# A fused attention and gated-MLP kernel: the hand-written order of all five engines is laid out anew

## Chip, core and metric

One core of one Trainium2 chip. The metric is device time in microseconds (us); less is better. The kernel before has a median of 278.79 us over three runs (279.18, 276.15 and 278.79).

## What is computed

Eight batches, twelve heads, 448 positions, head dimension 64. Queries and keys are RMS-normalised, then softmax attention, then a gated MLP with a spatial mix:

```python
q_n, k_n = rmsnorm(q, g_q), rmsnorm(k, g_k)
attn = softmax(q_n @ k_n.T / 8)                 # per head, 448 x 448
x = (attn @ v) laid out as (batch, 448, 768)
h = relu(x @ w_in)                              # 768 -> 1024
u, v = h[..., :512], h[..., 512:]
v_n = (v - mean(v)) / sqrt(var(v) + 1e-6)
v_s = w_spatial @ v_n + b_spatial               # mixes positions
out = (u * v_s) @ w_out                         # 512 -> 768
```

## The kernel before

All data of a batch is cut into 3 groups of 4 heads, so there are 24 groups G (batch G // 3). Nothing is scheduled by a compiler. A string, `PLAN`, is a list of 1,658 words; the kernel goes through it once, and each word issues the instructions of one step. Every engine runs its own instructions strictly in the order in which their words stand, and so do the DMA queues of SP (most transfers) and of POOL (the `v` and weight loads). Waits between engines come from the data and the buffers. A word is `name.arguments/slots/engine`; the engine is `a` (ACT), `v` (DVE) or `g` (POOL), and slots are buffer numbers: PSUM banks 0 to 7, or buffers of a pool (10 `raw`, 3 `sqt`, 4 `nrm`, 2 `kr`, 22 `et`, and so on).

The steps of a group G, with i = 0 for queries and 1 for keys:

- `L.G.i` loads q or k (SP, 448 KB), `Q` squares it into `sqt` (ACT, DVE or POOL), `R` sums the squares (DVE), `I` and `J` make 1/rms by a logarithm and an exponential (ACT), `N` multiplies into `nrm` (POOL or DVE). Group 0 has the same steps in two halves, in small letters (`l q r i j n p k`).
- The transpose to head dimension by position is done for groups 0 to 3 on TensorE (`P`, or `p`) with a copy out of PSUM (`K`, `k`), and from group 4 on by a DMA transpose on SP (`T.G.i`); `Z.G` then scales the transposed keys (DVE or ACT).
- `S.G.u` computes the scores of a seventh of the keys for the group's four heads (8 matmuls of 64x32 tiles; group 0 is cut otherwise), `E.G.u` is its exponential (ACT, PSUM to `et`). `s`, `a` and `b` sum those over the keys: `s` with ones, `a` and `b` with the two halves of V. From group 4 on two groups share these passes (`s.8.1.1` is for groups 8 and 9).
- `D` and `d` make the reciprocal of the sum (ACT), `X.G.half` multiplies (DVE, PSUM to `xt`). `v.b.n` is a load of a part of V of batch b (POOL, 112 or 224 KB).

The steps of a batch b: `V` and `W` (tail rows) and `U` are matmuls with `w_in`; `c` and `u` the relu copies out of PSUM; `B` the mean and variance; `M`, `m`, `A` the normalisation; `H` the spatial mix; `G` the gating; `O` the matmul with `w_out`; `o` its copy out of PSUM; `t.b.m` the store on SP (two DMAs of 64 rows each). `Y` and `y` transpose `w_spatial` at the start.

`z.n/f` issues n dummy matmuls of 64 columns on TensorE; nothing reads them.

[...]

```python
    def port(eng, inst):
        other = on_port.get("g" if eng is dve else "v")
        if other is not None:
            sync_dep(inst, other)
        on_port["v" if eng is dve else "g"] = inst
```

Of the kernel before, what the change touches and what calls it, by code (L numbers as in the profile page):

```python
# [27 lines left out]
y.0//a K.1.1/1/v S.1.5/45 S.1.1/23 Q.2.0/0/a R.2.0//v v.1.3//g L.2.1/5 S.1.6/67 Q.2.1/2/a wi.1.1//g E.1.5/2/a  # L28
wi.0.1//g Y.1/0 p.1.1/5 E.1.6/3/a R.2.1//v S.1.3/67 s.1.6.0/4 y.1//v k.0.1//v I.2//a wi.0.3//g E.1.1/4/a J.2//a
L.4.1/6 k.1.1//v E.1.3/5/a S.1.2/01 E.1.2/6/a s.1.5.0 a.1.1.0/5 S.0.3/23 s.1.3.0 N.2.1/2/v E.0.3/7/a S.1.4/67  # L30
E.1.4/8/a L.3.0/7 a.1.6.0 L.3.1/8 s.1.1.0 S.1.0/01 a.1.5.0 P.2.1/3 N.2.0/3/v P.2.0/2 L.6.1/9 wi.1.3//g wi.1.2//g
E.1.0/9/a Q.3.0/1/v S.0.6/67 K.2.1/2/v wi.0.0//g Q.3.1/0/g R.3.0//v s.1.2.0 b.1.1.0/3 S.0.2/01 b.1.6.0 a.1.2.0 s.1.0.0
wb Q.4.1/2/g K.2.0/2/v b.1.4.0 E.0.6/a/a s.1.4.0 R.3.1//v wi.1.0//g S.2.2/67 E.0.2/b/a D.1/0/a L.4.0/0 a.1.0.0 a.1.4.0
s.0.0.0/2 Q.4.0/1/v E.2.2/c/a S.0.4/01 E.0.4/d/a a.1.3.0 wi.0.2//g s.0.6.0 I.3//a s.0.1.0 b.1.0.0 L.5.1/3 d.1//a
Q.6.1/0/v b.1.2.0 X.1.0//v S.0.5/67 J.3//a v.1.1//g S.2.1/01 s.0.3.0 N.3.0/0/g s.0.2.0 b.1.3.0 a.0.6.0/4 a.0.1.0
b.1.5.0 E.0.5/e/a v.1.2//g X.1.1//v E.2.1/f/a S.2.0/56 E.2.0/g/a a.0.4.0 s.0.5.0 b.0.3.0/7 L.6.0/2 s.0.4.0 R.4.0//v
S.2.4/01 b.0.0.0 b.0.2.0 a.0.3.0 E.2.4/h/a b.0.5.0 L.7.0/1 a.0.0.0 a.0.5.0 L.5.0/5 s.2.1.0/6 S.2.3/01 b.0.1.0
Q.5.1/1/a P.3.0/5 R.4.1//v R.6.1//v N.3.1/1/g P.3.1/3 a.0.2.0 E.2.3/i/a Q.5.0/2/g S.2.6/01 K.3.0/3/v b.0.6.0 I.4//a
s.2.4.0 K.3.1/3/v D.0/1/a J.4//a E.2.6/j/a N.4.0/2/g b.2.1.0/5 L.7.1/4 S.3.0/23 R.5.0//v b.2.0.0 s.2.2.0 E.3.0/k/a
S.2.5/01 E.2.5/l/a R.5.1//v wx//v s.2.0.0 d.0//a T.4.0/1 s.2.3.0 b.2.6.0 b.2.2.0 s.2.6.0 X.0.0//v b.0.4.0 S.3.1/23  # L40
E.3.1/4/a b.2.4.0 a.2.0.0/0 s.2.5.0 a.2.5.0 a.2.3.0 a.2.4.0 I.5//a a.2.1.0 N.4.1/3/g T.4.1/0 S.3.4/12 D.2/0/a J.5//a
b.2.5.0 a.2.2.0 X.0.1//v E.3.4/3/a b.2.3.0 N.5.1/0/v T.5.1/1 S.3.3/34 N.5.0/1/g a.2.6.0 S.3.2/67 U.0.2.0/2 V.0.1.1/1
d.2//a V.0.1.0 X.2.1//v V.0.2.1/5 X.2.0//v V.0.1.2 T.5.0/0 U.0.2.1 Q.6.0/0/a U.0.2.2 R.6.0//v Z.4/1/v V.0.2.0
E.3.2/8/a S.4.2/67 E.3.3/9/a L.9.0/7 c.0.1//v I.6//a J.6//a N.6.1/2/g S.4.0/34 B.0.1//v u.0.2//a Z.5/0/v E.4.2/6/a
S.4.1/01 W.0/2 E.4.0/5/a E.4.1/2/a S.4.5/67 c.0.3//v S.4.4/34 E.4.4/1/a Q.7.0/2/v L.8.0/8 E.4.5/7/a V.0.2.2 c.0.2//v
U.0.0.0/2 U.0.0.1 S.5.6/01 E.5.6/0/a S.5.1/34 L.10.0/0 E.5.1/d/a U.0.0.2 U.0.3.2/5 U.0.3.1 S.5.0/67 u.0.0//v S.5.5/01
S.3.5/34 V.0.0.2/2 Q.7.1/1/g E.5.0/a/a U.0.3.0 V.0.0.0 E.3.5/b/a V.0.0.1 S.5.4/67 S.3.6/34 E.5.5/e/a s.3.0.0/1
R.7.1//v R.7.0//v I.7//a s.3.5.0 Q.9.0/0/g a.3.0.0/0 s.3.1.0 N.6.0/3/g s.3.2.0 Q.8.0/1/g L.11.0/6 u.0.3//v E.5.4/g/a
a.3.3.0 J.7//a S.5.2/56 B.0.2//v b.3.2.0/7 T.6.1/0 E.3.6/h/a s.3.3.0 a.3.5.0 E.5.2/f/a S.4.6/34 a.3.4.0 L.8.1/3
b.3.5.0 B.0.3//v c.0.0//v B.0.0//v s.3.6.0 E.4.6/l/a a.3.6.0 s.3.4.0 D.3/1/a b.3.0.0 a.3.2.0 S.4.3/56 T.6.0/2 S.5.3/23  # L50
L.10.1/5 N.7.1/0/g T.7.1/1 a.3.1.0 M.0//a E.4.3/c/a s.4.6.1/41 R.8.0//v v.2.2//g L.14.0/9 E.5.3/i/a s.4.1.1 m.0//a
Z.6/2/v N.7.0/1/g s.4.2.1 s.4.5.1 b.3.1.0 S.6.1/56 E.6.1/j/a A.0.1//v s.4.4.1 b.3.6.0 A.0.0//v A.0.2//v s.4.0.1
A.0.3//v s.4.3.1 b.3.4.0 b.3.3.0 d.3//a X.3.1//v D.4/0/a S.6.4/23 Q.8.1/2/g X.3.0//v U.0.1.2/5 U.0.1.0 U.0.1.1 H.0.0/4
E.6.4/b/a R.9.0//v G.0.0//v wo//g H.0.3/0 v.2.0//g G.0.3//v u.0.1//a H.0.1/6 S.6.3/23 S.6.0/45 b.4.6.1/07 b.4.4.1
b.4.0.1 d.4//a Z.7/3/a G.0.1//v D.5/1/a b.4.5.1 b.4.2.1 R.8.1//v b.4.3.1 a.4.4.1/61 E.6.0/k/a S.6.2/45 E.6.3/8/a
Q.10.0/1/g a.4.5.1 a.4.0.1 a.4.6.1 T.7.0/3 E.6.2/4/a d.5//a L.9.1/2 b.4.1.1 a.4.2.1 I.8//a R.10.0//v a.4.1.1 a.4.3.1
v.2.1//g S.7.0/23 X.4.1//v Q.10.1/0/g S.7.3/45 V.1.2.0/0 E.7.0/h/a X.4.0//v J.8//a N.8.1/2/g T.8.1/0 H.0.2/6 V.1.1.0/3
X.5.1//v X.5.0//v E.7.3/3/a G.0.2//v S.7.5/12 S.7.2/45 Q.9.1/2/v R.9.1//v S.7.4/67 V.1.2.2 E.7.5/9/a N.8.0/3/g
E.7.2/1/a V.1.2.1 T.8.0/1 c.1.2//a V.1.0.1/1 E.7.4/g/a L.11.1/4 V.1.0.0 V.1.0.2 W.1/045 S.6.5/67 c.1.0//a R.10.1//v
I.10//a o.0.3.1/0/v S.6.6/12 o.0.3.0//a c.1.3//v V.1.1.2 S.7.1/45 I.9//a J.9//a N.9.1/0/g T.9.1/1 U.1.1.0/0 U.1.1.2  # L60
E.6.5/7/a J.10//a E.6.6/e/a V.1.1.1 N.9.0/1/v U.1.0.1/7 S.7.6/12 U.1.1.1 Z.8/1/v E.7.6/5/a c.1.1//v U.1.0.0 U.1.0.2
O.0.1.0/6 E.7.1/a/a u.1.0//v u.1.1//v B.1.3//v S.8.1/12 S.8.3/34 s.6.0.1/57 E.8.1/0/a s.6.1.1 s.6.2.1 N.10.1/2/g
N.10.0/3/g s.6.3.1 B.1.0//v s.6.4.1 E.8.3/l/a s.6.5.1 s.6.6.1 T.9.0/0 S.8.2/01 U.1.3.0/2 U.1.3.1 Q.11.0/1/a Q.11.1/2/g
T.10.1/0 L.14.1/1 B.1.2//v U.1.2.0/3 D.6/0/a R.11.0//v B.1.1//v U.1.3.2 E.8.2/6/a O.0.1.1/4 u.1.3//v T.10.0/2
o.0.1.0/1/a U.1.2.1 d.6//a O.0.0.0/5 M.1//a D.7/1/a U.1.2.2 L.12.0/3 o.0.0.0/2/v o.0.1.1//a S.8.0/01 L.13.1/8 m.1//a
b.6.0.1/26 Z.9/0/v b.6.1.1 E.8.0/f/a b.6.2.1 u.1.2//v b.6.3.1 S.8.5/45 A.1.0//v b.6.4.1 L.13.0/2 d.7//a b.6.5.1
A.1.2//v b.6.6.1 E.8.5/2/a S.9.1/01 A.1.1//v O.0.0.1/7 X.7.1//v E.9.1/d/a L.12.1/7 Q.14.0/0/g L.18.1/5 S.9.4/34
# [689 lines left out]
```

## Time and profile before

The profiled execution took 275.98 us, of which its span (first to last instruction) is 274.2 us.

| | busy us of the span | instructions |
|---|---|---|
| TensorE matmul (PE) | 257.9 | 4372 |
| ScalarE (ACT) | 217.8 | 357 |
| VectorE (DVE) | 203.8 | 355 |
| GpSimd (POOL) | 145.0 | 122 |
| DMA, all queues | 51.14 MB, 187 GB/s mean | |

Durations of one instruction, from the groups of the page, that are used below:

| step | engine and form | mean ns |
|---|---|---|
| `E` | ACT, 128x896 out of PSUM | 923 |
| `N`, `Q` | POOL, 128x896 | 1691, 1683 |
| `N`, `Q` | DVE, 128x896 | 1088, 1086 |
| `R` | DVE | 1076 |
| `c`, `u` | DVE | 683, 619 |
| `c`, `u` | ACT | 591, 548 |
| `o` | DVE, ACT | 555, 491 |
| `Z` | DVE, ACT | 471, 1071 |
| `n` | DVE, POOL | 616, 950 |

How to read it: the span is a sum of stages with different limits. In the first 45 us attention of batch 0 is made, and no MLP matmul can start. From then to about 223 us attention of later batches and the MLP of earlier ones are interleaved. After that only MLP steps are left, and after 268.9 us only copies and stores. The busy time of PE is not PE at its peak, since matmuls overlap one another.

### The profile page before, as it was taken

Reading aid. Unit: us, or ns where it says so; the run is one execution under the profiler, and the core shown is the slowest. Engines: PE = TensorE matmul, PEld = TensorE weight load, DVE = VectorE, ACT = ScalarE, POOL = GpSimd, SP = SyncE. Lnnn points to the kernel's source line nnn. Section 1 sums busy time; section 2 is a strip of 40 time slices with the busy share of each in tenths; the row PEclk is TensorE's granted clock in tenths of the full one; section 3 lists DMA queues with packets and bytes.
Section 4 is the critical chain, followed back from the end, with each engine's and each line's share of the span. In section 5 each row is a group of like instructions: output and inputs, shape, how many; then the busy total and the mean of one; then the engine's idle time right before and its main releaser. Section 6 shows DMA issues by size and latency. Waiting matters only on the chain.

```text
span 274.2 us, 10148 instructions
## 1 busy us (share of the span) xinstructions
PE 257.9 (94%) x4372; PEld 137.5 (50%) x4389; DVE 203.8 (74%) x355; ACT 217.8 (79%) x357; POOL 145.0 (53%) x122
## 2 busy tenths in 40 slices
...
GB/s 208 319 344 273 260 171 119 295 204 245 167 145 168 376 177 187 198 251 184 232 184 267 286 246 241 175 95 61 194 114 141 117 2 2 31 29 115 154 279 204
DMA packets 63072, 51.14 MB, mean 187 GB/s; under 512 B 39601, under 2 KB 58674, under 8 KB 63026
## 3 DMA queue, kind: packets, MB, share of 16 engines
...
q8 instruction: 34, 0.56, 0.8%
q14 instruction: 12, 0.10, 0.1%
...
## 4 chain that ended last, share of the span: by engine, by line
PE 42%; POOL 13%; DMA 12%; DVE 10%; ACT 10%; issue 10%; SPq 1%; ACTq 0%; POOLq 0%; DVEq 0%
PE ps L551 8%; PE ps L690 7%; POOL nrm L438 7%; PE ps L662 7%; DMA vt<-in_v_dram 6%; ACT et L526 6%; PE ps L676 6%; PE ps L596 5%; PE ps L518 5%; POOL sqt L394 5%; DMA raw<-in_q_dram 3%; DVE ss L405 3%; DMA kr<-nrm 3%; PE ps L625 3%; POOL vt L326 2%
## 5 line engine op out<-in xcount | busy, mean ns | idle before, releaser
L526 ACT ACTIVATE et<-ps 128x896 bf16<-128x896 f32 x168 | 146.1, 923 | 13.4 <-PE ps L518 11.4
L438 POOL TENSOR_TENSOR nrm<-raw,rs 128x896 bf16<-128x896 f32 x40 | 67.3, 1691 | 29.0 <-ACT rs L423 9.4
L518 PE MATMUL ps<-qT,kT 64*32 64x448 bf16 x1344 | 61.1, 357 | 3.2 <-DVE kT L476 1.1
L551 PE MATMUL ps<-et,vt 64*32 64x448 bf16 x1344 | 52.1, 350 | 2.5 <-DMA vt<-in_v_dram 1.0
L394 POOL TENSOR_TENSOR sqt<-raw 128x896 f32<-128x896 f32 x28 | 46.8, 1683 | 13.8 <-DVE vn L653 9.3
L405 DVE TENSOR_REDUCE ss<-sqt 128x14 f32<-128x896 f32 x46 | 48.5, 1076 | 2.9 <-ACT sqt L392 1.2
L662 PE MATMUL ps<-xt,w_in 128*128 128x448 bf16 x192 | 43.4, 353 | 0.2
L518 PEld LDWEIGHTS <-kT 64*32 64x32 bf16 x1344 | 22.2, 90 | 31.7 <-issue 22.5
L690 PE MATMUL ps<-w_out,gt 128*128 128x384 bf16 x192 | 36.5, 326 | 0.1
L580 DVE TENSOR_TENSOR xt<-ps,rc 128x448 bf16<-128x448 f32 x48 | 27.9, 618 | 11.5 <-ACT rc L574 6.9
L596 PE MATMUL ps<-w_in,xt 128*128 128x512 bf16 x127 | 33.9, 380 | 0.9 <-issue 0.3
L551 PEld LDWEIGHTS <-vt 64*32 64x32 bf16 x1344 | 24.9, 92 | 16.2 <-issue 4.2
L373 ACT ACTIVATE os<-ps 128x384 f32<-128x384 f32 (+1 forms) x34 | 16.3, 491 | 15.2 <-PE ps L690 14.6
L551 PE MATMUL ps<-et,ones 64*32 64x448 bf16 x672 | 27.8, 349 | 0.0
L676 PE MATMUL ps<-w_spT,vn 128*128 128x448 bf16 (+1 forms) x128 | 27.7, 353 | 0.2 <-DVE xt L580 0.2
L662 PEld LDWEIGHTS <-w_in 128*128 128x128 bf16 x192 | 17.2, 97 | 20.8 <-issue 7.4
L690 PEld LDWEIGHTS <-gt 128*128 128x128 bf16 x192 | 18.1, 98 | 15.6 <-issue 2.7
L681 DVE TENSOR_TENSOR gt<-ps,us 128x448 bf16<-128x448 f32 x32 | 19.2, 619 | 9.0 <-PE ps L676 5.9
L637 DVE BATCH_NORM_STATS2 s<-vs 128x6 f32<-128x512 bf16 (+1 forms) x32 | 21.9, 683 | 1.6 <-ACT vs L587 1.1
L375 DVE COPY os<-ps 128x384 f32<-128x384 f32 (+1 forms) x30 | 16.5, 555 | 8.9 <-PE ps L690 5.5
L326 POOL DMA_DIRECT2D vt<-in_v_dram x34 | 23.0, 681 | 0.0
L589 DVE TENSOR_SCALAR vs<-ps 128x512 bf16<-128x512 f32 (+1 forms) x24 | 16.3, 683 | 7.4 <-PE ps L596 3.5
...
## 6 DMA issues: line engine op xcount, KB each, us to landing
...
w_in<-in_moe_w_in_dram POOLq DMA_DIRECT2D x8, 192.0 KB, 12.8
...
```

Source lines behind the costliest of these rows:

```text
L326: pool.dma_start(out=vts[b % 2][64 * halves[0]:64 * halves[0] + 64 * len(halves), g].rearrange("p r c d -> p r (c d)"), in_=src)
L394: port(eng, eng.tensor_tensor(out=t, in0=x, in1=x, op=ALU.mult))
L405: dve.tensor_reduce(out=sss[G % 3][:, i].rearrange("p r c -> p (r c)"), in_=sqt[where.pop(("sq", G, i))].rearrange("p r (c d) -> p (r c) d ...
L438: port(eng, eng.tensor_tensor(out=nrm[sl[0]].rearrange("p c r d -> p r c d"), in0=raw[where["raw", G, i]].rearrange("p r (c d) -> p r c d" ...
L518: pe.matmul(out=ps[at:at + 32, sl[n], 0:S], lhsT=kT[64 * r:64 * r + 64, c, 64 * hh + 32 * x:64 * hh + 32 * x + 32], rhs=qT[64 * r:64 * r + ...
L526: act.activation(out=ets[sl[0]], in_=ps[:, a:b + 1:b - a, 0:S], func=AF.Exp, bias=0.0, scale=1.0)
L551: pe.matmul(out=ps[32 * l:32 * l + 32, where[kind, G][0], 0:S], lhsT=w, rhs=et_of(G, r, c)[at:at + 64], start=(n == 1), stop=(n == C), til ...
L580: dve.tensor_tensor(out=xts[b % 2][:, 2 * g + half, :], in0=ps[:, where.pop(("ab"[half], G))[0], 0:S], in1=rcs[where["rc", G]], op=ALU.mult)
L596: pe.matmul(out=ps[:, bank, :], lhsT=xts[b % 2][:, j, 128 * m:128 * m + 128], rhs=w_in[:, j % 2, j // 2, DH:], start=(n == 1 and j == 2 * ...
L662: pe.matmul(out=ps[:, bank, 0:S], lhsT=w_in[:, j % 2, j // 2, 128 * f:128 * f + 128], rhs=xts[b % 2][:, j, :], start=(n == 1 and j == 2 * ...
L676: pe.matmul(out=ps[:, sl[0], 0:S], lhsT=vns[b % SLOTS["vn"]][rows, m, 128 * f:128 * f + 128], rhs=w_spT[rows, m, :], start=(m == 0), stop= ...
L690: pe.matmul(out=ps[:, sl[0], 0:384], lhsT=gts[b % 2][:, f, 128 * m:128 * m + 128], rhs=w_out[:, f, 384 * h:384 * h + 384], start=(f == 0), ...
```

## The change

The whole string `PLAN` is replaced by another order with the same 1,658 words; only the order, the slots and some engine letters differ, and the numbers in the `z` words. No other line changes. Counted by engine letter:

| step | before | after |
|---|---|---|
| `N` | 40 POOL, 6 DVE | 34 POOL, 12 DVE |
| `Q` | 28 POOL, 13 ACT, 5 DVE | 30 POOL, 9 ACT, 7 DVE |
| `n` | 2 POOL, 2 DVE | 4 DVE |
| `q` | 4 ACT | 3 ACT, 1 DVE |
| `k` | 4 DVE | 3 DVE, 1 ACT |
| `y` | 2 ACT, 2 DVE | 4 DVE |
| `Z` | 17 DVE, 3 ACT | 16 DVE, 4 ACT |
| `c` | 24 DVE, 8 ACT | 19 DVE, 13 ACT |
| `u` | 22 DVE, 10 ACT | 23 DVE, 9 ACT |
| `o` | 30 DVE, 34 ACT | 27 DVE, 37 ACT |
| dummies in `z` | 140 | 111 |

The diff, cut to the start, to some lines around batch 3's V loads, and to the end. Since every line of the string differs, words have to be looked for, not lines:

```diff
-setup//v l.1.0/0 gl.0//g z.1/f q.1.0/0/a l.0.0/1 z.5/f q.0.0/1/a z.11/f l.0.1 q.0.1//a z.1/f z.3/f z.11/f gl.1//g
-l.1.1 z.5/f z.1/f L.1.1/2 r.1.0//v r.0.0//v i.0//a L.1.0/3 j.0//a q.1.1//a gA//v z.1/f z.35/f r.0.1//v n.0.0//v
-Q.1.1/2/a z.34/f n.1.0//v z.9/f Q.1.0/1/a z.23/f r.1.1//v gB/2 gC//v i.1//a p.0.0/4 k.0.0/0/v p.1.0/0 k.1.0/0/v
-S.0.1/56 R.1.1//v ws//g R.1.0//v Y.2/1 y.2//v S.0.0/23 j.1//a Y.3/1 n.1.1//g v.0.1//g I.1//a J.1//a N.1.0/0/v Y.0/0
-P.1.0/4 N.1.1/1/v P.1.1/7 v.0.2//g L.2.0/4 v.1.0//g K.1.0/1/v E.0.1/0/a y.3//a E.0.0/1/a v.0.0//g n.0.1//g p.0.1/1
...
+setup//v l.1.0/0 l.0.0/1 q.0.0/0/a q.1.0/1/a r.0.0//v r.1.0//v i.0//a j.0//a n.0.0//v z.11/f z.24/f z.7/f z.5/f
+gl.0//g l.0.1 n.1.0//v l.1.1 q.0.1//a gl.1//g gA//v q.1.1//v r.1.1//v gB/3 L.1.1/2 r.0.1//v i.1//a Q.1.1/2/v L.1.0/3
+j.1//a z.13/f Q.1.0/1/a gC//v L.2.0/4 n.0.1//v z.20/f ws//g L.2.1/5 p.1.0/2 Q.2.0/0/a p.0.0/1 Y.2/0 R.1.1//v Y.3/6
+Y.0/3 k.1.0/0/v z.9/f v.0.1//g R.1.0//v y.2//v z.8/f R.2.0//v z.4/f k.0.0/0/a y.3//v S.0.1/45 y.0//v I.1//a z.3/f
+J.1//a Q.2.1/2/a R.2.1//v v.0.2//g S.0.0/01 N.1.0/0/g P.1.0/2 E.0.0/0/a v.1.0//g N.1.1/1/v v.0.0//g I.2//a J.2//a
+P.1.1/6 K.1.0/1/v L.4.1/6 K.1.1/1/v p.0.1/7 L.3.0/7 Q.3.0/1/g z.3/f S.1.1/01 L.3.1/8 k.0.1//v L.6.1/9 S.1.6/23
...
-v.3.4//g U.2.2.1 c.2.0//v E.10.4/i/a U.2.2.2 Z.12/1/v v.3.2//g O.1.0.0/0 T.13.1/1 u.2.2//v E.11.6/0/a N.14.0/2/g
...
-O.1.1.0/3 v.3.3//g L.18.0/8 E.11.4/6/a U.2.1.2 Q.17.1/1/g o.1.1.0/0/v S.11.5/45 s.10.0.1/06 u.2.1//v s.10.1.1
...
+o.0.1.0/1/v N.10.0/1/g v.3.4//g u.1.1//v s.6.4.1/60 s.6.3.1 s.6.0.1 s.6.2.1 E.6.5/k/a s.6.5.1 T.9.0/1 S.8.3/12 Z.9/1/v
...
+v.3.3//g J.12//a E.8.5/c/a U.1.2.0/7 U.1.2.1 A.1.3//v X.6.1//v U.1.2.2 S.9.4/12 a.6.6.1/30 a.6.2.1 A.1.1//v o.0.0.1//v
...
-t.6.0 o.7.0.0/3/a O.7.2.0/3 o.7.0.1//a O.7.2.1/5 t.7.0 o.7.2.0/0/a O.7.1.0/1 o.7.2.1//a O.7.1.1/4 t.7.2 o.7.1.0/1/v
-W.8/70 o.7.1.1//a t.7.1 o.7.3.0/4/a o.7.3.1//a t.7.3
...
+o.7.0.1/3/a t.6.2 o.7.0.0//a o.7.2.1//v t.7.2 t.7.0 W.8/56 o.7.3.1/4/v o.7.3.0//a O.7.1.1/7 o.7.1.1/1/a t.7.3
+O.7.1.0/0 o.7.1.0//a t.7.1
```

At the start, SP issues its first 13 transfers in the same order as before (`l.1.0 l.0.0 l.0.1 l.1.1 L.1.1 L.1.0 L.2.0 L.2.1 L.4.1 L.3.0 L.3.1 L.6.1 wb`). The first words of the other engines, in order, are now: ACT `q.0.0 q.1.0 i.0 j.0 q.0.1 i.1 j.1 Q.1.0 Q.2.0 k.0.0 I.1 J.1 Q.2.1 E.0.0`, DVE `r.0.0 r.1.0 n.0.0 n.1.0 gA q.1.1 r.1.1 r.0.1 Q.1.1 gC n.0.1 R.1.1 k.1.0 R.1.0 y.2 R.2.0 y.3 y.0 R.2.1 N.1.1 K.1.0 K.1.1`, POOL `gl.0 gl.1 ws v.0.1 v.0.2 N.1.0 v.1.0 v.0.0 Q.3.0`. Before they were: ACT `q.1.0 q.0.0 q.0.1 i.0 j.0 q.1.1 Q.1.1 Q.1.0 i.1 j.1 I.1 J.1 E.0.1`, DVE `r.1.0 r.0.0 gA r.0.1 n.0.0 n.1.0 r.1.1 gC k.0.0 k.1.0 R.1.1 R.1.0 y.2 N.1.0 N.1.1 K.1.0 K.1.1`, POOL `gl.0 gl.1 ws n.1.1 v.0.1 v.0.2 v.1.0 v.0.0 n.0.1`.

247 lines of the change are left out of this document (123 added, 124 removed).

## Prediction

> **What bounds the kernel now.** I first read the page's busy times, then the busy times by stage.
>
> ```profile
> PE 257.9 (94%) x4372; PEld 137.5 (50%) x4389; DVE 203.8 (74%) x355; ACT 217.8 (79%) x357; POOL 145.0 (53%) x122
> ```
>
> ```profile
> 11.60:45.10 33.50, 30.56 (x564) 20.00 (x565) 28.73 (x36) 30.74 (x50) 23.98 (x25) 0.90 1.02 253
> 45.10:223.40 178.30, 173.62 (x3214) 86.00 (x3226) 140.36 (x246) 162.25 (x262) 118.54 (x89) 1.00 0.96 192
> 223.40:268.90 45.50, 45.31 (x439) 23.85 (x434) 27.61 (x56) 19.02 (x37) 0.00 (x0) 1.00 0.36 100
> 268.90:274.20 5.30, 0.00 (x0) 0.00 (x0) 0.00 (x0) 0.97 (x2) 0.00 (x0) 0.85 0.59 195
> ```
>
> The columns are the stretch, its length, then the busy time of PE, PEld, DVE, ACT, POOL, the granted clock, the DMA share and GB/s. PE is idle for 2.9 us from 11.6 to 45.1, 4.7 us in the 178 us after it, and 0.2 us then. So the orders of the other engines can win only the start, these 4.7 us and the tail; PE's own work is the same, dummies apart. In the first stage ACT (92% of it) and DVE (86%) are nearly as full. I then read the start on ACT, DVE and POOL.
>
> ```profile
> 8.44 0.95 ACT L392 ACTIVATE sqt<-raw 128x896 f32<-128x896 f32 x1 [0.48 <-DMA raw<-in_k_dram]
> 11.71 0.95 ACT L392 ACTIVATE sqt<-raw 128x896 f32<-128x896 f32 x1 [2.31 <-DMA raw<-in_q_dram]
> ...
> 19.56 1.73 ACT L526 ACTIVATE et<-ps 128x896 bf16<-128x896 f32 x2 [0.91 <-PE ps L518]
> ```
>
> ```profile
> 14.47 2.10 DVE L438 TENSOR_TENSOR nrm<-raw,rs 128x896 bf16<-128x896 f32 x2 [0.40 <-POOL nrm L446]
> ...
> 17.66 0.68 DVE L476 TENSOR_SCALAR kT<-ps,g_col 128x896 bf16<-128x896 bf16 x1
> ```
>
> ```profile
> 13.18 0.94 POOL L446 TENSOR_TENSOR nrm<-raw,rs 128x448 bf16<-128x448 f32 x1 [9.59 <-ACT rs L431]
> 14.06 2.93 POOL L326 DMA_DIRECT2D vt<-in_v_dram  x4
> ```
>
> `Q.1.0` holds ACT until its load lands at 11.7; `n.1.1` on POOL waits 9.6 us for `j.1` behind it, and four V loads wait behind `n.1.1`. The group-1 exponentials begin at 19.56. Last come the waits for late transfers and the tail.
>
> ```profile
> DVE kT L476 <- DMA kr<-nrm: 3.3, 3, 2.4
> PEld L551 <- DMA vt<-in_v_dram: 1.9, 2, 1.2
> ```
>
> ```profile
> 268.90 0.99 ACT L373 ACTIVATE os<-ps 64x384 f32<-64x384 f32 x2 [0.28 <-PE ps L625]
> 270.18 1.18 SPq L711 DMA_DIRECT2D out_dram<-os  x2
> ```
>
> PE waits 1.9 us in all for V; DVE waits 3.3 us for transposed keys. After the last matmul two copies run in a row on ACT, and `t.7.3` is issued only at 270.18, after `t.7.1`.
>
> **The change, part by part,** against the profiled 275.98 (1.78 outside the span).
>
> *Load of the engines.* From the engine letters and the mean durations: POOL -6x1.69 +2x1.68 -2x0.95 = -8.7 us. DVE +6x1.09 +2x1.09 +2x0.62 (`n`), about +0.6 (`q`, half a `Q`), +2x0.39 (`y`), +0.62, -0.47, -5x0.68, -3x0.56, -0.65 (`k`) = +5.8. ACT about +0.5. Over the whole span DVE then has 64 us idle and ACT 56, so this is free after 45 us. Before 45 us it isn't: up to `X.2.0`, which frees batch 0's MLP, DVE gets 2 `R`, 2 `n`, 2 `y` and a `q` more and a `k` less: 2.15+1.24+0.78+0.6-0.65 = +4.1. ACT's work up to there is the same within 0.1.
>
> *Start.* By hand, in the new order: `Q.1.0` 11.7 to 12.65; `Q.2.0` (its load lands at 12.8 by the trace's landing records) to 13.8; `k.0.0`, now on ACT behind both and 1.0 long (my estimate, between 0.95 of a `Q` and 1.07 of a `Z` on ACT), to 14.8; `I.1`, `J.1` to 15.3; `N.1.0` on POOL to 17.0; `N.1.1` on DVE after `R.2.1` to 18.4; `P.1.1` 0.7, `K.1.1` 0.68; first group-1 scores 20.0, exponentials 20.6 against 19.56: +1.1. The POOL queue no longer has `n.1.1`, so `v.0.1` and `v.0.2` are issued from 3.6 us instead of 14. The loads of 448 KB land 1.22 us apart here (12.8, 14.0, 15.2), and the `w_spatial` load of 392 KB, alone on POOL's queue, goes with a gap of 3.2 us between the landings at 8.4 and 11.6. So two V loads cost `L.2.0` and `L.2.1` something between 0 and 2.4; I take 1.1. [...] Against it, the dummies are spread up to the scores instead of all ending at 7.9 us, so that the granted clock may not fall (0.66 in 10 to 20 us); the two transposes `P.1` took 0.66 and 0.74 there and `P.2` 0.39 and 0.44 later, so at most -0.6, which I take. [...] Start: +1.1+1.1-0.6 = +1.6. Ends: -1 (DVE's 9.3 us idle before 45.1 hide everything, and the first exponentials no longer sit behind a load) and +4.1 (DVE idles as long as before).
>
> *PE's work.* 29 dummies fewer: nothing, they ended at 7.9 in a wait for loads. Changes between 64x32 tiles and full-width matmuls: 107 before, 104 after; at 0.3 (22.5 us of waits in 61 score groups is 0.37) -0.9 to 0; I take -0.5.
>
> *Late transfers.* With PE's queued work as a ruler (count times the spacing of each step), a V load stood 15 us ahead of its first use in the median, now 27; loads with less than 8.6 us (what the late one at 115.3 took) were six, now two. `v.3.3`, waited for at 122.7, moves from 6.9 to 36 us ahead; `v.5.2` and `v.5.3`, waited for at 179.3, from 8 and 9 to 19 and 33. The 1.9 us go. From the end of `N` to the first use of its transpose there were 11.2 us in the median, now 15.2; I take 1.0 of the 3.3 us for PE, since DVE's wait of 2.4 up to 182.6 ended together with a PE gap of 1.2. Together -2.9; ends 0 (what is next waits, mostly a bank to be emptied) and -5.
>
> *New tight spots.* `v.3.1` has 3.5 us by the ruler, though on POOL it stands right behind `N.11.0` and may start earlier; `T.16.1` 3.0 and `T.22.0` 4.4 from their `N`. At the medians of the trace (6.3 a V load, 4.8 a transpose) that is 2.8+1.8+0.4 = 5.0 if all come last, 0 if SP and POOL run ahead; I take 0.6. SP moves loads past transposes too: `L.16.1` is issued only 3 us ahead of `Q.16.1`, which makes POOL wait, not PE.
>
> *Tail.* Last is now `O.7.1.0`, one copy (0.49) and `t.7.1`, instead of two copies and a store behind `t.7.1`: -0.5 and some 0.3 of SP, against 192 KB instead of 96 (3.2 to 2.4 us to landing): -0.5; ends -0.8 and +0.3.
>
> *Sum:* +1.6 -0.5 -2.9 +0.6 -0.5 = -1.7, so 274.3 for an execution like the profiled one. Before's median stands 2.8 above that execution; if the spread comes from landings, half of it stays (my estimate): +1.4, 275.7.
>
> **Rivals.** *(1) DVE at the start becomes the bound, slower.* Place: DVE between 12 and 45 us, which takes over `N`, `n` and `Q` from POOL and in the port order waits for POOL's 1.69 us steps. It was busy 22.3 of 25.1 us from 20 on, so 2.8 us of idle can't hold 4.1 more unless it goes in before 20. Price at full +4.1; with the transfers' gain lost behind it, 278.8+4.1-0.5-0.5 = 281.9. It decides once `X.2.0` ends after 48 us (45.1 before). Against it: the extra small steps stand early, where DVE waited (6.5 us idle before 20).
> *(2) Nothing moves.* PE is 97% busy from 45 to 223 us; removed waits come back as waits for the next bank or exponential, and the start costs its +1.6: 275.98 +1.6 -0.5 and before's 2.8 with some of it kept, 278.5.
> *(3) Landings were all of it.* Start at its low end, transfers -4, before's offset gone: 275.98 -1 -0.5 -4 -0.5 +1.0 = 271.
>
> **The numbers.** Forecast 275.7: 0.50, of it 0.10 above 276.0. Rival 1: 0.20. Rival 2: 0.20. Rival 3: 0.10. About 1% (2.8 us) is what three runs can tell from no change, as the runs of before spread over 3 us. Faster, under 276.0: 0.40+0.10 = 0.50; within: 0.10+0.20 = 0.30; slower, over 281.6: 0.20. The range goes from rival 3 to rival 1, 271 to 282 (each has about half of its chance outside, and a little of the forecast is); the likeliest case's own is 272.5 to 278.5.
>
> **What would show it.** In the new profile: group-1 exponentials near 20.6 to 21.7; `X.2.0` near 46.5; no `PEld L551 <- DMA vt` in the waits; a granted clock above 0.66 in 10 to 20 us; the span's end under 5 us after the last matmul. Wrong would be: `X.2.0` after 48, waits of PE for V or keys as long as before, or PE idle over 5 us between 45 and 223.

## The result, and the profile after

The changed kernel takes 278.17 us (median of 22 runs), the kernel before 276.05 (22 runs beside them): a ratio of 1.008, 95% interval 1.006 to 1.0099. It is slower by 2.1 us, where 275.7 and faster was forecast. The three runs of before that were shown, with their median of 278.79, lay above what 22 of them give; the profiled execution of before, 275.98, was typical. That of after took 277.57.

The busy times of the whole span, then of stretches with the same meaning as those of before (to the end of `X.2.0`, to 223.4, to the last matmul, the rest; columns as there):

```profile
PE 260.3 (94%) x4360; PEld 136.9 (50%) x4360; DVE 207.9 (75%) x359; ACT 217.8 (79%) x359; POOL 136.1 (49%) x116
```

```profile
11.60:47.30 35.70, 33.15 (x592) 20.38 (x590) 32.61 (x43) 30.68 (x50) 24.26 (x23) 1.00 1.12 286
47.30:223.40 176.10, 174.97 (x3247) 86.08 (x3246) 140.96 (x244) 163.83 (x266) 107.91 (x83) 1.00 0.96 190
223.40:268.90 45.50, 45.50 (x430) 24.15 (x428) 27.76 (x56) 18.53 (x37) 0.00 (x0) 1.00 0.29 78
268.90:275.80 6.90, 0.05 (x1) 0.00 (x0) 0.00 (x0) 0.79 (x2) 0.00 (x0) 0.82 0.68 214
```

Attention of batch 0 now ends at 47.34 instead of 45.06 (+2.3). From there to the last matmul it is 221.6 us instead of 223.8 (-2.2), and the last matmul ends in the same place, 268.95 against 268.87. Behind it stand 6.84 us instead of 5.33 (+1.5). The three make the 1.6 between the two profiled executions. So three questions: what the start lost, what the middle won, what the tail lost.

The start, on ACT and on POOL's queue:

```profile
12.91 0.95 ACT L392 ACTIVATE sqt<-raw 128x896 f32<-128x896 f32 x1 [3.01 <-DMA raw<-in_q_dram]
15.38 0.95 ACT L392 ACTIVATE sqt<-raw 128x896 f32<-128x896 f32 x1 [1.52 <-DMA raw<-in_q_dram]
16.24 0.90 ACT L373 ACTIVATE qT<-ps 64x896 bf16<-64x896 bf16 x1
...
23.28 0.92 ACT L526 ACTIVATE et<-ps 128x896 bf16<-128x896 f32 x1 [0.92 <-PE ps L518]
```

```profile
3.52 1.47 POOL L326 DMA_DIRECT2D vt<-in_v_dram  x2
17.68 1.69 POOL L438 TENSOR_TENSOR nrm<-raw,rs 128x896 bf16<-128x896 f32 x1 [12.69 <-ACT rs L423]
```

The two V loads are issued at 3.5 us, among the q and k loads. `Q.1.0` gets its load at 12.9 instead of 11.7 and `Q.2.0` its own at 15.4, where 12.8 was the landing before; `k.0.0` stands behind it, `N.1.0` on POOL behind `I.1` and `J.1`, and the first exponential of group 1 is at 23.28 (19.56 before).

TensorE at the start:

```profile
1.68 2.69 PE L261 MATMUL ps<-ident 128*128 128x64 bf16 x47 [1.68 <-POOL ident masks.py:199]
7.66 0.58 PE L384 MATMUL ps<-one_f,g_row 1*128 1x1 f32 x2 [3.29 <-DVE g_row L379]
8.17 1.94 PE L261 MATMUL ps<-ident 128*128 128x64 bf16 x33
```

From start to start the dummies stand 53 ns apart, at 2 us and still at 8. Before, they ran unbroken to 7.9 us, 53 ns apart up to 6.4, where the first record of the granted clock starts (1.00), and 29 ns apart behind it; here `gB` waits 3.3 us for the gains. The granted clock is printed as 1.00 from the span's start, but the trace has no record of it before 24.09 us, and the durations say half rate up to there: the dummies at 22.4 us still stand 53 ns apart, and the seven transposes of `P.1.0` take 0.93 us, as before (0.92), where the record has 0.50 from 13.2 to 20.0 us; those of `P.2.1` take 0.56 at 27.6 us, at a granted clock of 1.00.

Waits for transfers, and the tail on SP:

```profile
ACT sqt L392 <- DMA raw<-in_q_dram: 6.6, 4, 3.0
DVE kT L476 <- DMA kr<-nrm: 1.7, 1, 1.7
```

```profile
259.39 10.55 SPq L714 DMA_DIRECT2D out_dram<-os  x14
...
268.82 0.87 ACT L373 ACTIVATE os<-ps 128x384 f32<-128x384 f32 x2 [0.76 <-DMA out_dram<-os]
270.04 1.20 SPq L711 DMA_DIRECT2D out_dram<-os  x2
271.33 1.19 SPq L714 DMA_DIRECT2D out_dram<-os  x2
```

No line of PE waiting for `vt` is left, and the wait for transposed keys is 1.7 instead of 3.3. At the end the copy of `o.7.1.0` is done at 269.69, but its store goes out at 271.33, behind others.

### The profile page after: what moved, and what is told of

It reads as the page before. It is cut to its first block, busy times and chain, and to the rows that moved or that the text cites. A ratio compares the mean times of both kernels' runs of the same rounds, so it can differ in the third digit from the quotient of the medians.

```text
span 275.8 us, 10107 instructions
## 1 busy us (share of the span) xinstructions
PE 260.3 (94%) x4360; PEld 136.9 (50%) x4360; DVE 207.9 (75%) x359; ACT 217.8 (79%) x359; POOL 136.1 (49%) x116
## 4 chain that ended last, share of the span: by engine, by line
PE 57%; ACT 13%; DVE 9%; DMA 8%; issue 4%; POOL 4%; SPq 3%; ACTq 0%; POOLq 0%; DVEq 0%
PE ps L551 12%; PE ps L662 10%; ACT et L526 10%; PE ps L596 9%; PE ps L518 8%; PE ps L690 7%; PE ps L676 7%; DMA raw<-in_q_dram 4%; DMA out_dram<-os 3%; PE ps L625 3%; DVE ss L405 3%; POOL sqt L394 3%; DVE nrm L438 2%; SPq L714 2%; DVE us L589 1%
## 5 line engine op out<-in xcount | busy, mean ns | idle before, releaser
L438 POOL TENSOR_TENSOR nrm<-raw,rs 128x896 bf16<-128x896 f32 x34 | 57.1, 1685 | 48.7 <-ACT rs L423 22.1
L518 PE MATMUL ps<-qT,kT 64*32 64x448 bf16 x1344 | 59.3, 361 | 2.3 <-ACT qT L373 1.5
L394 POOL TENSOR_TENSOR sqt<-raw 128x896 f32<-128x896 f32 x30 | 50.0, 1674 | 15.5 <-DVE vn L653 5.1
L551 PE MATMUL ps<-et,vt 64*32 64x448 bf16 x1344 | 48.7, 349 | 0.7 <-ACT et L526 0.4
L518 PEld LDWEIGHTS <-kT 64*32 64x32 bf16 x1344 | 21.2, 90 | 31.1 <-issue 23.4
L596 PE MATMUL ps<-w_in,xt 128*128 128x512 bf16 x144 | 35.9, 380 | 0.0
L551 PEld LDWEIGHTS <-vt 64*32 64x32 bf16 x1344 | 23.7, 92 | 14.5 <-issue 3.3
L373 ACT ACTIVATE os<-ps 128x384 f32<-128x384 f32 (+1 forms) x37 | 17.8, 492 | 14.8 <-PE ps L690 7.5
L676 PE MATMUL ps<-w_spT,vn 128*128 128x448 bf16 (+1 forms) x128 | 27.6, 353 | 0.0
L375 DVE COPY os<-ps 128x384 f32<-128x384 f32 (+1 forms) x27 | 14.7, 554 | 12.1 <-PE ps L690 3.6
L596 PEld LDWEIGHTS <-xt 128*128 128x128 bf16 x144 | 13.0, 98 | 16.7 <-issue 3.7
```

The costliest lines, as they stand in the source:

```text
L394: port(eng, eng.tensor_tensor(out=t, in0=x, in1=x, op=ALU.mult))
L438: port(eng, eng.tensor_tensor(out=nrm[sl[0]].rearrange("p c r d -> p r c d"), in0=raw[where["raw", G, i]].rearrange("p r (c d) -> p r c d" ...
L518: pe.matmul(out=ps[at:at + 32, sl[n], 0:S], lhsT=kT[64 * r:64 * r + 64, c, 64 * hh + 32 * x:64 * hh + 32 * x + 32], rhs=qT[64 * r:64 * r + ...
L551: pe.matmul(out=ps[32 * l:32 * l + 32, where[kind, G][0], 0:S], lhsT=w, rhs=et_of(G, r, c)[at:at + 64], start=(n == 1), stop=(n == C), til ...
L596: pe.matmul(out=ps[:, bank, :], lhsT=xts[b % 2][:, j, 128 * m:128 * m + 128], rhs=w_in[:, j % 2, j // 2, DH:], start=(n == 1 and j == 2 * ...
L676: pe.matmul(out=ps[:, sl[0], 0:S], lhsT=vns[b % SLOTS["vn"]][rows, m, 128 * f:128 * f + 128], rhs=w_spT[rows, m, :], start=(m == 0), stop= ...
```

## The experiments

Each was timed beside the kernel before (276.3 to 277.3 us in the five comparisons); ratios are to it, with 95% intervals. The changed plan's ratio to compare with is 1.008 (1.006 to 1.0099).

### The start

**V loads late.**

```diff
-z.9/f v.0.1//g R.1.0//v ... R.2.1//v v.0.2//g S.0.0/01 N.1.0/0/g
+z.9/f R.1.0//v ... R.2.1//v S.0.0/01 N.1.0/0/g v.0.1//g v.0.2//g
```

> The changed plan with two words moved: v.0.1 and v.0.2 stand behind N.1.0 on POOL, so they are issued near 17 us and not at 3.5. Theory A (the V loads delay the q and k loads, and with them the start): L.1.0 lands near 11.6 instead of 12.9, L.2.0 near 12.8 instead of 15.4, L.2.1 near 14.0 instead of 16.8; the first group-1 exponential comes 1.5 to 2.5 us before 23.28, X.2.0 as much before 47.34, and the time falls by 1.2 to 2.3. Rival B (DVE, which was given more early work, bounds the stage up to X.2.0): the loads land early just the same, but X.2.0 moves by less than 0.7 and the time by less than 0.7. Rival C (the landings are set by something else): L.2.0 stays at 15 or later and nothing moves.

Measured: 278.40, ratio 1.0053 (1.0021 to 1.0085). ACT in its profile:

```profile
11.50 0.95 ACT L392 ACTIVATE sqt<-raw 128x896 f32<-128x896 f32 x1 [1.49 <-DMA raw<-in_q_dram]
12.71 0.95 ACT L392 ACTIVATE sqt<-raw 128x896 f32<-128x896 f32 x1 [0.26 <-DMA raw<-in_q_dram]
...
21.46 0.92 ACT L526 ACTIVATE et<-ps 128x896 bf16<-128x896 f32 x1 [0.62 <-PE ps L518]
```

Both loads are back in time, group 1 gains 1.8 us and `X.2.0` 1.5 (45.86). That is theory A, and rival B falls: DVE does not bound this stage. Yet the time hardly follows. In this profile, which is 1.1 us above the kernel's median, the last matmul is later than in the changed plan's (270.97 against 268.95), and the loss is in one place: the first scores of group 4, ahead of which PE stands for 2.1 us,

```profile
41.04 3.27 SPq L493 DMA_TRANSPOSE kr<-nrm  x1
...
49.78 0.45 DVE L476 TENSOR_SCALAR kT<-kr,g_col 128x896 bf16<-128x896 bf16 x1 [3.92 <-DMA kr<-nrm]
...
50.29 0.57 PE L518 MATMUL ps<-qT,kT 64*32 64x448 bf16 x16 [2.12 <-DVE kT L476]
```

as `T.4.1` lands no earlier than it did. Behind the wait, in this execution, the granted clock was 0.50 from 51.31 to 54.73 us: six `w_in` matmuls took 2.29 us instead of 1.48 and 24 scores 1.32 instead of 0.76, together 1.4 us. A second chain lay close behind the first.

**Loads behind the first transposes.** Where the kernel before issued `T.4` and `T.5` at 40 to 47 us and its next loads after them, the changed plan has `L.12.1`, `L.10.0` and `L.9.1` ahead of `T.4`. SP of before, and of after:

```profile
40.15 1.33 SPq L493 DMA_TRANSPOSE qT<-nrm  x1
41.79 3.24 SPq L493 DMA_TRANSPOSE kr<-nrm  x2
```

```profile
37.88 3.13 SPq L493 DMA_TRANSPOSE qT<-nrm  x1
41.10 3.46 SPq L493 DMA_TRANSPOSE kr<-nrm  x1
```

The issue of `T.4.1` holds SP for 3.5 us instead of 1.2 (the second line of before holds `T.4.1` and `T.5.1`), and from 40 to 50 us the transfers moved 239 GB/s at a DMA share of 1.16, before 117 GB/s at 0.79.

```diff
-L.12.1/8 ... L.10.0/7 ... T.4.0/1 ... T.4.1/0 L.8.0/6 ... T.5.1/1 ... T.5.0/0
+T.4.0/1 ... T.4.1/0 L.8.0/6 ... T.5.1/1 L.10.0/7 ... T.5.0/0 L.12.1/8
```

> The changed plan with L.10.0 moved behind T.5.1 and L.12.1 behind T.5.0 on SP, so that they no longer stand ahead of the first DMA transposes. Theory D (the changed plan put loads of 448 KB ahead of T.4, the transfers are saturated there, the two transposes of group 4 take 3 us each to be issued instead of 1.2, the last lands near 49, and the first scores of group 4 wait for them): T.4.0 and T.4.1 are issued in 1.2 to 2.2 us each, Z.4 ends before 48.5, the wait ahead of S.4.5 (0.46 us in the profile of the changed plan, 2.5 in two other executions) is under 0.5, and the median falls by 0.5 to 2.0. Rival (the transposes are slow by themselves in this place, or the two loads come late for Q.10.0 and stop POOL): Z.4 ends as late as now, or POOL stands ahead of Q.10.0 and PE loses later what it gained; time the same within 0.5.

Measured: 277.63, ratio 1.0003 (0.9962 to 1.0044), an interval clear of the changed plan's: the time speaks for theory D, with some 2 us (1 to 3 by the two intervals). The profiles show about half of it. In all six executions with the loads behind, the issues of `T.4` took 1.3 to 1.7 and 1.9 to 2.8 us (here 1.4 and 2.6) and PE's matmuls had no wait ahead of `S.4.5`. In all eight with the loads ahead, the issues took 3.1 to 4.6 and 3.3 to 3.5 us, and PE waited 0.1 us in the changed plan's profile, 0.3 to 0.6 in four others and 1.6, 2.1 and 2.3 in three: 1.0 in the mean. Where the other half lies is open. `Z.4` was not earlier in the one profiled execution (50.9, the whole 277.76 us), as its start was later by itself: `L.1.0` landed 1.2 us later than in the changed plan's profile. There the expectation missed, and by 0.4 us with the second issue.

**k first on ACT.**

```diff
-p.1.0/2 Q.2.0/0/a p.0.0/1 ... R.2.0//v z.4/f k.0.0/0/a y.3//v
+p.1.0/2 p.0.0/1 ... z.4/f k.0.0/0/a Q.2.0/0/a R.2.0//v y.3//v
```

> The changed plan with Q.2.0 behind k.0.0 on ACT (R.2.0 behind it in the plan; DVE's own order stays). Theory A (ACT's order at the start costs, since k.0.0 and group 1's I and J stand behind a square whose load lands at 15.4): k.0.0 ends near 14.8 instead of 17.1, I.1 and J.1 near 15.6 instead of 17.6, N.1.0 ends near 17.3 instead of 19.4. But N.1.1 stands behind R.2.1 on DVE, which still waits for L.2.0 and L.2.1, so the first group-1 exponential gains only 0.3 to 1.0 and the time falls by 0.2 to 1.0. Rival (N.1.1 is held by I and J, not by R.2.1): group 1 and the time gain about 2.

Measured: 277.66, ratio 1.0022 (0.9988 to 1.0056). In its profile the first exponential of group 1 is at 22.98 (0.3 earlier) and `X.2.0` ends at 47.09, so the low end of the theory; that the time fell by 1.6 is more than this explains, and the interval is wide.

**The three together.**

> The three start edits together: v.0.1 and v.0.2 behind N.1.0, Q.2.0 behind k.0.0, L.10.0 and L.12.1 behind T.5. Theory A with D (the start can give back 1.5 to 2 us, but only if the transposes of group 4 don't come last instead): X.2.0 ends 1.5 to 2.5 us before 47.34, the wait ahead of S.4.5 is under 0.7, and the median falls by 1.5 to 3.0, to below the kernel before. Rival (something behind 50 us takes it back again): X.2.0 as early, the time lower by less than 0.7.

Measured: 276.19, ratio 0.9969 (0.9936 to 1.0003). `X.2.0` ends at 45.94, `Z.4` at 48.20, and SP issues the transposes of group 4 in 1.3 and 1.9 us:

```profile
36.49 1.33 SPq L493 DMA_TRANSPOSE qT<-nrm  x1
39.44 1.90 SPq L493 DMA_TRANSPOSE kr<-nrm  x1
```

The start's loss is undone but for 0.9 us, and the plan is then 1.1% below the changed one.

**Dummies in the gap.**

```diff
-z.7/f z.5/f
+z.7/f z.5/f z.90/f
```

> The changed plan with 90 more dummies ahead of gB, where TensorE stood idle from 4.21 to 7.66 us. Theory (that gap keeps TensorE at half rate until 24.09 us): the clock is raised between 6 and 9 us; dummies after it stand 29 ns apart and not 53, the transposes P.1 take 0.4 to 0.5 instead of 0.67, and scores of group 0 about 0.35 instead of 0.53 us a matmul; since loads and ACT set the start, the first group-1 exponential gains only 0.2 to 0.9 and the time falls by 0.1 to 0.9. Rival 1 (the clock falls again in the waits from 10 to 24 us, so that the dummies before 8 us help nothing): transposes as slow as now, time the same. Rival 2 (gB, gC and the first transposes come late behind the dummies): up to 0.5 slower.

Measured: 283.01, ratio 1.0188 (1.0134 to 1.0243). The clock was raised at 6.7 us, the weight loads of a transpose of group 0 took 0.42 us instead of 0.72, but at 13.5 it fell again and those of `P.1` took 0.67 as ever: rival 1, as far as the clock goes. None of the three explains a time 1.1% (3 us) above the changed plan's. The profile does: three new stops of PE, of 1.3, 2.3 and 0.6 us, behind 96, 165 and 210 us. The longest,

```profile
164.70 1.13 PE L551 MATMUL ps<-et,vt 64*32 64x448 bf16 x34
168.10 1.13 PE L551 MATMUL ps<-et,vt 64*32 64x448 bf16 x38 [2.27 <-issue]
```

stands in the middle of a pass, where no instruction waits for a semaphore ("issue").

### The middle: packets of instructions

The kernel before has two such stops:

```profile
72.86 0.37 PE L518 MATMUL ps<-qT,kT 64*32 64x448 bf16 x5 [0.72 <-issue]
...
182.38 0.56 PE L551 MATMUL ps<-et,vt 64*32 64x448 bf16 x14 [0.76 <-issue]
```

Among the transfers is a queue of kind "instruction", with packets of 16 KB (here the changed plan's; number, MB, share of the DMA engines' time):

```profile
q8 instruction: 34, 0.56, 0.9%
```

The kernel has 4,360 weight loads and as many matmuls, 8,720 TensorE instructions; over 34 packets that is some 256 for each and, as an estimate from these numbers, 64 bytes an instruction. So I take the queue for TensorE's. The packets' times beside stops of PE in which no semaphore was waited for (the last matmul's start; the packet's start + the time it took):

```
run            last matmul at  packet          PE goes on, us after the packet's end
before         71.8            70.6 + 0.97     1.26
before         181.3           179.8 + 1.16    1.38
90 more        96.5            95.6 + 0.98     1.48
90 more        165.5           165.9 + 0.96    1.28
90 more        210.1           208.0 + 1.55    1.39
three together 104.1           102.7 + 0.94    1.35
```

Each ends 1.3 to 1.5 us after a packet. So theory F, a reading of these times: TensorE ran out of instructions. The counts bear it out. In the five traces with such stops in which no record of TensorE is missing, the records ahead of the eight stops number 3,265 (once), 5,569 (three times), 5,825 (three times) and 7,361 (once): each is a multiple of 256 and 193 more, in both orders and with five numbers of dummies. And 90 more dummies, as well as 128 more, make the 34 packets 35. So dummies count too, and by theory F 90 more move the packets' borders by 180 instructions against the work. The test is to move them by a whole packet:

```diff
-z.7/f z.5/f ... z.4/f
+z.7/f z.5/f z.90/f ... z.42/f
```

> The changed plan with 128 more dummies (90 ahead of gB and 38 more in z.4), that is 256 more TensorE instructions, where the run with 90 more was 1.9% slower than the kernel before, with stalls of TensorE at 96, 165 and 210 us in which no semaphore is waited for and which end 1.3 to 1.5 us after a 16 KB packet of TensorE's instruction queue. Theory F (TensorE's instructions come in packets of 16 KB, 256 instructions, and late packets stop it; 180 more instructions moved the packets' borders to bad places): 256 more put the borders back to the same work, the three stalls are gone, and the time is that of the changed plan within 1.0 (277 to 279.5). Rival (the dummies cost time by themselves, by the clock or by what they delay): stalls and time stay as with 90, near 283.

Measured: 278.03, ratio 1.0034 (1.0003 to 1.0065). The three stops are gone (one of 0.55 at 43 has come), and 38 more dummies made the kernel 1.5% (4 us) faster: the dummies' own time is not what cost. But then the 29 dummies that the change itself took out matter, and the middle's gain may be theirs. From both sides:

```diff
 # the kernel before
-z.34/f
+z.5/f
 # the changed plan
-z.7/f z.5/f
+z.7/f z.5/f z.29/f
```

> The kernel before with 29 dummies fewer at the start (z.34 is z.5), so with the changed plan's number of 111 and its borders of instruction packets; nothing else. Theory F (late instruction packets stop TensorE, and where their borders fall decides): the two stalls without a semaphore at 71.8 and 181.3 us (0.9 us each) move or go, others may come, each ending 1.2 to 1.5 us after a packet has landed; the time changes by up to 2 in either direction. Rival (the stalls belong to the steps where they stand): both stay in their place. The clock at the start may fall: then up to 1 slower before 25 us, whatever the packets do.

> The changed plan with 29 more dummies ahead of gB, where TensorE is idle from 4.2 to 7.7 us: the kernel before's number of 140 and so its borders of instruction packets (58 instructions further), and nothing else moved. Theory F (the changed plan's middle is quick since its packets happen to come in time, not since its order is proof against late ones): stalls without a semaphore come, 0.5 to 3 us in all, each 1.2 to 1.5 us after a packet, and the time rises by 0.5 to 3, ratio to the kernel before 1.010 to 1.019. Rival (the new order stands late transfers of every kind): the ratio stays at 1.008 within 0.3%, or falls a little by a better clock.

Measured: the kernel before with 111 dummies 275.18, ratio 0.9968 (0.9934 to 1.0001); the changed plan with 140, 280.57, ratio 1.0118 (1.007 to 1.0166). The first interval reaches 1 and the second overlaps the changed plan's, so the times alone don't decide. In the traces the first run has no stop of this kind left, and the second has one of 2.0 us:

```profile
171.78 0.56 PE L518 MATMUL ps<-qT,kT 64*32 64x448 bf16 x13 [2.00 <-issue]
```

and it met the late keys of group 4 (1.6 us ahead of `S.4.5`), which are no matter of packets. By stages, from the profiled executions:

| plan | dummies | `X.2.0` ends | from there to the last matmul | behind it |
|---|---|---|---|---|
| before | 140 | 45.06 | 223.8 | 5.33 |
| before | 111 | 45.37 | 221.1 | 5.41 |
| before | 95 | 45.21 | 222.2 | 5.45 |
| changed | 111 | 47.34 | 221.6 | 6.84 |
| changed | 140 | 48.06 | 225.2 | 5.47 |
| changed | 201 | 47.78 | 226.5 | 6.29 |
| changed | 239 | 48.22 | 221.5 | 6.06 |

With the same number of dummies the old order's middle is as quick as the new one's in these executions, 221.1 against 221.6. These are single ones: that of before with 111 took 273.70 us, the lowest of its twelve (median 275.18), so of its gain of 2.7 only about 0.9 is in the medians (0.3%).

**The V loads.** The rest of the middle's gain should be the waits for V, 1.9 us.

```diff
 # the kernel before, first try
-v.3.0//g ... v.3.3//g ... v.5.1//g ... v.5.3//g ... v.5.2//g
+v.3.0//g v.3.3//g ... v.5.1//g v.5.3//g v.5.2//g
 # second try
-v.4.1//g ... v.3.3//g ... v.4.3//g ... v.5.3//g ... v.5.2//g
+v.4.1//g v.3.3//g ... v.4.3//g v.5.3//g v.5.2//g
```

> The kernel before with its V loads v.3.3, v.5.2 and v.5.3 issued early, v.3.3 behind v.3.0 and the others behind v.5.1. Theory (the middle gain of the changed plan is the waits for these loads): no wait of PE for vt is left (1.9 us in the profile of before), and the time falls by 1.0 to 2.0. Rival F (much of the middle gain is that packets of TensorE's instructions came in time): the stalls at 71.8 and 181.3 us stay, 0.9 us each, and the time falls by less than 0.7, as what waited for V now waits for something else.

> The kernel before with v.3.3 behind v.4.1 (near 103 us instead of 115) and v.5.2 and v.5.3 behind v.4.3 (near 152 instead of 171), so that in POOL's queue they no longer stand ahead of v.4.3, for which the first try of this waited 1.7 us at 159. Theory V (waits for V are worth what they last): no wait of PE for vt over 0.3, the stretch from 110 to 185 us shorter by 1 to 2, and the time lower by 0.7 to 2.0. Rival (the transfers are saturated there, and a V load that goes earlier makes another transfer late): another wait of PE for vt, kr or an instruction packet of 0.7 to 2, time the same within 0.7.

> The kernel before with 111 dummies instead of 140 and with v.3.3 behind v.4.1, v.5.2 and v.5.3 behind v.4.3. Theory V (late V loads cost the kernel before 1 to 2 us, and in the two tries they were hidden by packets of instructions that came late): without those packets' stalls the gain shows, 0.7 to 2.0 below the run with 111 dummies alone (ratio 0.9968), that is 0.990 to 0.994. Theory F alone (what the middle can win is the packets' stalls): the same as that run within 0.7, ratio 0.994 to 1.000. If it is above 1.000, the loads that go earlier make other transfers or packets late.

Measured, in this order: ratios 1.0034 (1.0000 to 1.0068), 1.0048 (1.0016 to 1.0081) and 0.9969 (0.9939 to 0.9998). In the first, PE waits 1.6 us at 160 for `v.4.3`, which now stood behind the loads moved. In the second that is cured, and two stops without a semaphore have come (1.1 us at 160.5, 0.5 at 167.7). In the third, on top of 111 dummies, the loads win nothing over 111 dummies alone (0.9968). And with 111 dummies alone, every V load in its old place, PE's wait for V was

```profile
PEld L551 <- DMA vt<-in_v_dram: 0.4, 1, 0.4
```

and with 95 dummies there was none. So theory V falls: of the 1.9 us in the profile of before, most belonged to that execution and not to the plan.

### The tail

**Stores on other queues.** First `t.6.1`, `t.6.2` and `t.7.2` on POOL; then `t.6.2`, `t.7.2` and `t.7.0` on POOL and the second half of `t.7.1` on ACT, alone and with the three start edits; then the same without ACT's.

```diff
-t.6.2 ... t.7.2 t.7.0 ... t.7.1
+t.6.2//gg ... t.7.2//gg t.7.0//gg ... t.7.1//sa
```

> The changed plan with t.6.1, t.6.2 and t.7.2 (six of the last stores) issued by POOL, which has nothing to do from 223 us on, instead of SP. Theory (SP's queue of stores, one DMA after another at 0.55 to 0.6 us, sets the tail): SP is free when t.7.1's data are ready at 269.7, both of its stores are issued by 270.4 instead of 271.9, the span's end comes 1.0 to 1.6 us earlier, 5.3 to 5.8 after the last matmul instead of 6.85, and the time falls by 1.0 to 1.6. Rival (the transfers themselves are the limit, 0.68 of the DMA engines' time in the tail, 192 KB more at the end): the issues come early but the last landing moves by less than 0.5.

> The changed plan with the tail edit alone: t.6.2, t.7.2 and t.7.0 issued by POOL, the second half of t.7.1 by ACT. Theory (SP's issuing sets the tail): t.7.1's first half is issued within 0.2 us of its data, the span ends 5.2 to 5.8 us after the last matmul instead of 6.85, and the median falls by 1.0 to 1.6 to 0.3 to 0.5% above the kernel before. Rival: the last landing moves by less than 0.5, and the time with it.

> The three start edits (v.0.1 and v.0.2 behind N.1.0, Q.2.0 behind k.0.0, L.10.0 and L.12.1 behind T.5) and the tail: t.6.2, t.7.2 and t.7.0 issued by POOL, the second half of t.7.1 by ACT. Theory (start and tail add up): the tail behind the last matmul is 5.2 to 5.8 us instead of 6.5 to 6.8, and the time is 0.8 to 1.5 below the run with the start edits alone (276.2), near 275, below the kernel before by 0.5 to 1.0%. Rival (the transfers, not SP's issuing, set the tail): tail 6.2 or more, time as with the start edits alone.

> The three start edits and t.6.2, t.7.2 and t.7.0 issued by POOL; t.7.1 stays on SP, since ACT took 2.2 and 3.4 us to issue the only transfer it was given in the tail. Theory (SP's queue of stores sets the tail, ACT's first issue spoilt the last two tries): t.7.1 is issued within 0.2 us of its data, the tail behind the last matmul is 5.2 to 5.7 us against 6.2 with the start edits alone, the time 0.3 to 1.0 below that run, ratio to the kernel before 0.990 to 0.997. Rival (the transfers set the tail): tail 6.0 or more, ratio 0.997 or above.

Measured: ratios 1.0037 (1.0006 to 1.0069), 1.0130 (1.0075 to 1.0185), 1.0045 (1.0008 to 1.0083), 1.0010 (0.9979 to 1.0042); behind the last matmul 6.09, 7.43, 6.65 and 6.58 us, against 6.84 in the changed plan and 6.21 with the three start edits alone. None reaches the 5.2 to 5.8 that was expected. The first comes nearest, with a time 0.4% below the changed plan's and intervals that overlap. ACT's single issue took longer than two of SP's:

```profile
268.44 2.20 ACTq L714 DMA_DIRECT2D out_dram<-os  x1
```

and with ACT left out, SP did issue `t.7.1` 0.03 us after its data, but its two issues took 0.8 and 0.9 us instead of 0.55 to 0.6, the last transfer ended 2.2 us behind them, and the end did not come sooner. In that run, with stores on two queues, the transfers held the end: that far the rival holds. By the packets' records they moved some 250 to 320 KB in each of the eight us from 265.8 to 273.8 in the changed plan.

It does not explain the changed plan's own tail. In all ten profiled executions of the new order with its stores on SP alone, the last transfer ended 1.7 to 1.8 us after SP's last issue, so SP's queue set the end. And SP was late where one of its issues met a packet and took until after its end; I call this a held store. In the changed plan the first store of `t.6.0` held SP from 260.64 to 262.87, TensorE's packet ran from 260.61 to 262.49, and from there to `t.7.1` SP issued without a pause. In the chain that ended last it stands as

```profile
260.91 1.96 SPq L714
```

The longest issue of a store from 10 to 5 us ahead of the last matmul, beside the tail:

| plan | longest issue | behind the last matmul |
|---|---|---|
| changed | 2.23 | 6.84 |
| V loads late | 2.10 | 6.72 |
| k first | 1.79 | 6.42 |
| three together, 95 dummies | 1.74 | 6.43 |
| three together | 1.62 | 6.21 |
| changed, 239 dummies | 1.21 | 6.06 |
| loads behind | 1.11 | 5.77 |
| three together, 127 dummies | 0.60 | 5.42 |
| changed, 140 dummies | 0.59 | 5.47 |

(With 201 dummies the packet came at 270.79, a store was held for 1.39 us, and the tail was 6.29.) So of the 1.5 us that the tail lost, nearly all is the held store: where none was held, the new order's tail is 5.4 to 5.5 and that of before 5.33. This is read from traces that differ in more than the held store; no run changed it alone. The old order has more room for it. With stores held for 1.70 and 1.51 us its tails were 5.41 and 5.45 (111 and 95 dummies), with one held for 2.27 it was 6.04 (111 and V early). In the changed plan SP, held, still had 15 stores to issue from 6.1 us ahead of the last matmul on, before 11; where no store was held, the new order had 12 there too.

### Versions with other borders

The three start edits with 16 dummies more or fewer, and the kernel before with 95:

> The three start edits, with 16 more dummies in the idle gap ahead of gB (127), so that every border of TensorE's instruction packets moves by 32 instructions, and the packet that began at 260.4 us, in the middle of the last stores, begins about 1 us earlier. Theory F: the stalls without a semaphore come at other places than 104 us, the store that meets the late packet is another or none, and the time moves by up to 1.5 either way from the ratio 0.997 of the start edits alone. Rival (borders don't matter within a packet): 0.997 within 0.2%.

> The three start edits, with 16 dummies fewer (95): borders of the instruction packets 32 instructions the other way. Theory F: as with 127, other stalls, the time up to 1.5 either way from the ratio 0.997. Rival: 0.997 within 0.2%. With fewer dummies TensorE's clock at the start is half in any case, so that the start stays.

> The kernel before with 95 dummies instead of 140 (z.34 is z.5, z.23 is z.7): borders 90 instructions from before and 32 from the run with 111. Theory F: where 111 had no stall and a ratio of 0.9968, this has other places for its packets; by F alone nothing says whether they are good, 0.990 to 1.008, and each stall without a semaphore ends 1.2 to 1.5 us after its packet. If the time is below that of 111, it is the best version so far.

Measured: with 127 dummies 275.06, ratio 0.9939 (0.9908 to 0.9969); with 95 dummies 277.18, 0.9983 (0.9946 to 1.0019); the kernel before with 95, 275.45, 0.9950 (0.9917 to 0.9982). The first is faster than both kernels, by 0.6% and some 1.4%. Its profiled execution, 278.42, had a stop of 2.3 us without a semaphore at 166, with a granted clock of 0.50 for 3.4 us behind it, and is not typical of it. The plan with 127 and the one with 95 differ in nothing but the borders and the dummies' own time in a gap, and their intervals overlap a little; that borders matter within a packet is likely, and these runs alone don't prove it. Nor do they show the new order to be the better one: the old one with 95 dummies (0.9950) is within the interval of the new one with its three start edits and 127 (0.9939).

## Why the prediction was wrong

Between the two profiled executions the sum said -1.7 us and the traces say +1.6. Of the 3.3 us between them the tail has 2.0, the start 0.7 and the middle 0.6. The steps that failed are the tail, taken at -0.5 where +1.5 was measured; the start's delay by V loads, taken at 1.1 where the load of `L.2.0` came 2.6 later; and, by the medians, a term that was not in the sum, loads ahead of `T.4`. Moving these loads and the start's words back took the plan from 1.008 to 0.9969.

**Start, forecast +1.6, measured +2.3.** The mechanism of the V loads was right and its size wrong: 1.1 was taken, where `L.2.0` landed 2.6 us later (15.4 against 12.8), more than the 2.4 at which the range named ended, and moving the V loads back returned 1.8 at group 1. The -0.6 for the clock was wrong, and no run shows the term: the new dummies left a gap of 3.3 us and still stood 53 ns apart at 22.4 us, the first record of the clock is at 24.09, and 90 more dummies only raised it for some 7 us (6.7 to 13.5), without an earlier start (`X.2.0` at 47.78). Group 1 came at 23.28 where 20.6 to 21.7 was named; `X.2.0` at 47.34, near 46.5 and under the 48 of rival 1. Moving the V loads back took that rival out: DVE was not the bound. (The port order that it names is the kernel's own function `port`, an order between steps of DVE and of POOL; no trace or run shows what would happen without it.)

**Not in the sum: loads ahead of `T.4`.** That SP's loads had been moved past transposes was noted for `L.16.1` alone, and taken to make only POOL wait. For `T.4` it cost some 2 us in the median (1.008 to 1.0003 without it); the waits of PE that the profiles show make 1.0 of it in the mean.

**PE's work, "29 dummies fewer: nothing, they ended at 7.9 in a wait for loads".** This step was wrong in kind, though it is not what turned the sign. Their time was hidden, but they are 58 instructions, and so, at some 256 instructions a packet, every border of TensorE's packets moved. Taken out of the kernel before alone, they gave a ratio of 0.9968; put back into the changed plan, 1.0118 instead of 1.008, with a stop of 2.0 us without a semaphore in the middle of the profiled execution. Both intervals leave room for no effect, but both point to fewer dummies being the faster here, and the old order with 95 dummies is clear of 1 (0.9950). The -0.5 for tile changes could not be separated from it.

**Late transfers, forecast -2.9, middle measured -2.2.** With the -0.5 and the +0.6 the forecast for the middle is -2.8: near in sum, by luck. The waits for V are gone, as forecast, but three tries of moving those loads won nothing, and with 111 dummies the old order shows 0.4 us of them. Of the two stops of 0.7 and 0.8 at 72.1 and 181.6, both ending 1.3 to 1.4 us after a packet, the second was put down to late keys.

**New tight spots, forecast +0.6.** None shows: no wait of PE for `vt`, and DVE's one wait for keys (1.7, for `Z.16` at 139) ended 8 us ahead of `S.16.0`.

**Tail, forecast -0.5, measured +1.5.** Only the last copy and the last store were counted, as if SP were free for them. In the profiled execution a packet held a store for 2.23 us and SP's queue did not catch up before the end. Where no store was held, the new order's tail was 5.42 and 5.47: even there the -0.5 did not come.

**Offset, +1.4.** Three runs were read as a median that stands 2.8 above the profile; 22 runs put it at the profile. So 275.7 looked faster beside 278.79, and beside 276.05 it would have been no change. The +1.4 is a term that no run bears out.

Rival 2 gave the nearest time, 278.5, though not its reason: things moved by 1.5 to 2.3 us in three places and cancelled in part.
